# VectorE's exponential with a half-octave cubic, in a new order of the attention kernel

## The chip, the core and the metric

The kernel runs on one core of one Trainium2 chip. The metric is device microseconds of one execution; three timed executions gave a median of 3478.04 us (3476.9 to 3479.99). A trace of one profiled execution tells where the time goes. The engines are TensorE (PE in the profile; its weight loads are PEld), VectorE (DVE), ScalarE (ACT), GpSimd (POOL) and SyncE (SP), which issues DMAs.

## What is computed

Four layers of grouped attention with one key and value head (two sets of weights, used in turn), each with a layer norm before it and a residual sum behind it. There are 2048 rows of width 512, 32 query heads of width 16:

```python
def _A_ref(x, wq, wk, wv, wo):          # H = 32, Dh = 16, S = 2048
    q = (x @ wq).reshape(B, S, H, Dh).transpose(0, 2, 1, 3)
    k = x @ wk
    v = x @ wv
    scores = jnp.einsum("bhqd,bkd->bhqk", q, k) * (Dh ** -0.5)
    p = _softmax(scores, axis=-1)
    o = jnp.einsum("bhqk,bkd->bhqd", p, v)
    return o.transpose(0, 2, 1, 3).reshape(B, S, H * Dh) @ wo
x = A_x
x = x + _A_ref(_layernorm(x), *A);  x = x + _B_ref(_layernorm(x), *B)
x = x + _A_ref(_layernorm(x), *A);  x = x + _B_ref(_layernorm(x), *B)
```

The exponentials of the scores are by far the largest part: 4 layers x 32 heads x 2048 x 2048 of them.

## The kernel before

**Tiles of exponentials.** The scores are cut into 4096 tiles of 128 partitions x 1024 columns. TensorE makes a tile of scores in PSUM, one engine turns it into exponentials in SBUF (`pt`, 16 buffers), and TensorE multiplies these by the values and a column of ones and sums them in two PSUM banks `acc` (the ones give the softmax's denominator).

- 3715 tiles go through ScalarE: `score` (L767) makes a tile in one of two PSUM buffers `st`, and one ACTIVATE at L777 takes the exponential. In what follows such a tile is a **score tile**.
- 381 tiles go through VectorE: `score_v` makes half a tile in the bank `by_v`, `exp_first` (L800) turns it into an integer whose upper bits are the exponent of the result (L809, twice a tile), and then a chain of six passes over 1024 columns follows: cut out the mantissa (L823), keep the exponent (L825), three passes of a polynomial in the mantissa (L826 to L828), and the product (L820). VectorE takes such tiles 24 ahead of ScalarE.

**TensorE in eighths.** The matmuls of attention work on 64 x 32 parts of the array: two halves of 64 rows, and in each four columns of 32. Each half does its own work; below they are half 0 and half 1. `both` (L482) issues four matmuls on a half at a time, at L495. The kinds of steps are:

- the score tile: one group of four on each half;
- a sum into `acc`: `acc[0]` on half 0 only, `acc[1]` on half 1 only, 256 columns, or 512 where the same sum's next step follows at once (`carry` in `step`, L875). These are float32 and stream twice;
- a product step: a piece of a projection (queries, keys and values, outputs) summed into the one bank `beside`, on either half. A product has 12 steps on each half.

**The touch.** The two halves must not sum into one bank at the same time. Where a product goes from one half to the other, `touch` (L904) has VectorE copy one column of `beside` into `seen` (L906): VectorE waits until TensorE has written the bank, and TensorE's next write to `beside` waits for VectorE's copy. All engines run their own instructions in order.

**The order.** `ORDER` (L56) is a string, written out by hand or by a program; the kernel walks it letter by letter, and each letter issues one step: `S` a score tile; `a` to `s` steps on one or both halves (table `STEPS`, L201: for `a` a sum on both halves; `l` a sum on half 0, `m` on half 1; `p` a product step on half 0, `q` on half 1; `b` to `k` mixtures, `r` and `s` half a VectorE tile); `P` and `F` steps on the whole array; `Y` a touch; `I` VectorE's first pass; `0` and `1` the next pass of one of two chains under way; `X`, `G`, `D` VectorE's other work; `Q` a load of queries. So a piece `SaaY0` is a score tile, two sums on both halves, a touch and a pass of a chain.

GpSimd squares queries and keys for a check of their lengths (L440, L416) and takes powers for the layer norm (L376).

Of the kernel before, what the change touches and what calls it, by code (L numbers as in the profile page):

```python
# [11 lines left out]
I32 = mybir.dt.int32  # L12
AF = mybir.ActivationFunctionType
ALU = mybir.AluOpType
# [35 lines left out]
LEAD = 1013283008.0  # L50
C0, C1, C2, C3 = 37.67991256713867, 23.053848266601562, 12.310662269592285, -0.15703019499778748
# [5 lines left out]
    "SSXPPPSPPPQSaSPPPSPPPSXaSXaaSbpSaaSbSbbSpppSaaYScSccScSccSaXQSXamGSmSGFSXlaXSaXXSaXXaSXaXSXaXaSaSamXSXFS"  # L57
    "XaSXQaaXSaSFSXaXSaXSGFGSlXXaXSaSFSXaaXSaSbbSbpSbbSapSaYSQaaScqSaaScGSccSqGqqSmXaXSaXSaXaXSFSXaXXaXSXXaSX"
    "aXaXSXlXXSaaXXSSQaaSXXSFSXaXSaXSGFGSgXaISaXSfXaISFX0SXa0SaXaS0aSF0SaaXSa0SQaaXSa0SbbSlGpSlbGSkbISbSrYaIS"
    "c0c0Sqc0Scc0SeSaXaXSa0SFaXS0QaSaaXSXaaXXSmXGSmXXmXSlXGSgXaISaXXSaXXaSXfXISa0aS0mXSaXa0SFS0aSQaXaS0aSaXaS"  # L60
    "XGSFG0SlaSXaSXafXSIFXSXsaISaXa0Sa0SF0SaaXSa0SQaXSa0aSb0pSalGSppGSbhSIbSkdISaY0aS0c0qScc0ScSc0aSqaXSaXa0S"
    "aQSaXaXSXFSXaXaXXSXmGqSGqcSicIScSjcISaY0mS0bp0Saa0SbpSb0Saa0SQbSbaXSaXaSaSacGSqjGSmIaSiISaa0Sc0q0SccS0aS"
    "aaY0Sbb0SbSQbbSapSpaXSaXaSlGpSkaISbGpShbISb0pS0a0SaaS0cScc0Scc0ScSQaaYSpaXSaXaSaSbbSgGpISpbGShbISd0Sa0aY"
    "0SaSc0cSc0qScc0SaSQeaXSaXSaaSaaSFGSXfSIaXcGSgISa0aS0ap0SaaS0bSaa0SbbXS0bSQaXaSXbDpXSaaYScGScqqGSjqISaaDS"
    "iISaXa0SaXqS0aaXS0mSaXaSXSaaSQaXXSaDSXaaD0SPPPSGPPGSPDrSaIaDS0aSas0SaaISPP0Sf0aISaD0SgaISa0SQaa1Sa0rSaa1"
    "SPGPSGPPDSaXaDSaXSaDppDS0bpSaIl0SakSaIp0SaSh1p0SaaS1aD0SccSIcq0SioISc0SfaYDSa0SbdDSaXaDSaXSaD0aSbpISb0b0"
    "SkbISb0SaaY1Si0qSaa1Sc0SaaD1Scc0ScScIaXSa0SaaXSaDa0SFSaXrDSaIbDSh0SaaISpb0Sg0aISb0Sbb1Sa0Saa1Sj0cScc1Scq"
    "0ScSaIaXSa0SQaaXSa0sSbaISa0kSbGpSGpppISpa0Sh0aISa0Saa1Si0qSccD0ScSc1c0SaSaYIaSD0dSaXa0SfaSIaXSa0aShpDSb0"
    "bSbISb0b0Sa0sSaaYISa0Sfc1Sc0qSaa1Sc0SccISa0qSaaXSa0SaaXSa0kSbIpSb0hSbIpS0a0Sa0aSiqISa0aSi1qSa0Saa1S0bSaY"
    "aISq0cSc0jSaaISc0SaaXSa0SaaXSr0mISQa0SF0SaaXSXaSPPPSPPGPSGsPISaXX0SaaS1a0Saa1Sa0SaaXSa0aSaXSaaXSa0SaPXSf"  # L70
    "aISl0SaaXSP0PSasXSaaISaXSa0aSXrPSaIaXSPSaaSXsXSaIa0SP0PPSa1Sa0rSaa1S0PPPSa1SPPP0SaaISa0SgaISPP0PSaXSa0aS"
    "hpISb0b0Sa0SgaISc0qSic1Sa0Saa1Sb0pSbpISaaY0SjcISc0qSQaaXSa0Shb1Sb0bSaISlGl0SpbGSb0mSaY0SicISc0qSfa1Sc0Sa"
    "aISc0c0SaSaXaSXXaDSaXXaDSaXXSaDXaXSa0sSaIaSXD0mSaaX1Sf0SaaISXaXSF00SaSaXaDSaXSgXmISaD0SflDSFD0SaaXS0SSIa"
    "XSaXaXD0SF0SXaS0aaSXsaISF0SaaXSa0SaaXSa0ShbIS0pa0SaDaS0kbSbIpSDb0rSalYDSc0SQaa1Sc0SaaISa0a0ScScGqqGSqq0S"
    "aaXSaXSaDXa0SaSaX0aSFXSsDaXISaXa0SXa0SaXX0fScIqSc0qScaDS0aSgaISDb0kSbbISbDpS0b0Sa0aSraISc0cSaXSa0aSaXaS0"
    "fScIcS0qc0Sa0sSaaISb0Shb1Sb0pSa1aS0aScIcS0eSaa0SsaISb0bSaXSa0aSaXrSaIa0Sc0Sc0cSm0SgaISb0pShb1Sa0SaaISQc0"
    "qq0ScSa0aSsaISbGpkGSpp0SaaXSa0SaaISaXSaDa0S0jcISc0qScc1Sj0aSa1Sa0aSb1pSaa0SbSbIbD0SkbSIaaY0SiSaXa0SaaISa"
    "XSaDa0SF0SaXa0SjcSIcq0Sic1Sm0Saa1Sb0pSbbISb0ShbISa0SaaY1Sa0Sic1SaXa0SaScIc0SqcSj0cSaaIS0aShb1S0bSaIaS0bb"
    "0SkbISa0SaaYS1Qgq0SeaXSa0SbaISlGpSl0bGSb0ShbISa0pSha1Sa0SaaY1Sc0SaaISc0cSc0SiaSIc0qSaaXSa0ShbISb0pSk0aIS"
    "a0aSa1Si0cScq1Sc0cSc1SaaY0SapSbIb0SaSaXaXXSrDaISaXXaSDaSXXgmDXSXa0SamXS1aXD0SamISa0SaXrSIaaXS0FSaXSa0aSa"  # L80
    "XrSXaDaS0FSXSDXSXXDSF0SISaXa0SaXsSQaIa0Sa0SF1SaXaS0aSaXaS0arSPGPPGSP0PSPPPISa0SaD0aSsaISa0aSaD1Sa0aSa1Sa"
    "0aSa0SfaISP0PSaaDSa0SaaD0SasSaIaDSa0Sg0aISPP0SaaXSaXSa0aSaX0SaaSXa0rSaaISXFS0faISXl0SaX0aSsXSIaaXX0SrSa1"
    "a0SaS1a0SaaIS0SgaISm0Sf1Sa0aSa1Sa0aSlISa0SsaISa0aSr1SQa0aS1Sa0aSGSGlISa0SgaISaD0Saa1Sa0SaaD1Sf0SaaIS0mSa"
    "0SgaISa0SgaDSm0SaaISDm0SaDaS0jcISc0Scc1Sj0qqSaaY1Sb0Sbb1Sbb0SbSaIaXSa0SicISc0Sic1Sa0qSaIaS0qa0SjaSIaq0Sa"
    "aS1a0ShbS1bp0SbbISb0SaaXSa0sSccISc0Sia1Sa0aScISa0a0SjcSaImY0SQhSa1a0Saa1SbGpSpGppS0pbSaIa0SbSaXaDS0scScI"
    "cS0cSi1cSD0aqSaIaY0Sa0ShbSIb0pSgbDSb0SbaXSaXXaDSaXXSaDaXXSa0SalISaXXSa0aXS0fISaX0aSa1Sa0rSaaXSXl0SFSXa0S"
    "aaISaXaSXa0Sa0Sas0SaaISF0SrSX0SISaXaSXaX0Sa0a0SasSaIa0SFS1aXSa0aSaXSa0aSF0SQaXa0SaSaXa0SajSGqqqGScIc0SaS"
# [103 lines left out]
    "mD0Sa0SasSIaa0SaSD1ar0Saa1S0SaaIS0SaaDSs0SaaISaD0SarSDaa0SSIa0aS0sSIa0aSa1Sa0rSaa1S0Saa1SS0aaSI0SaaS0asS"  # L191
    "aISa0fSIlS0ag0SImS0aaS1rS0aaS1aS0aSa1aS0SaaIS0sSaIaS0aSa1rSa0aSISa0a0SsSIaa0SrSGGSl0aSa1Sa0aSaISaD0aS0mS"
    "a0aSsaDISa0Saa1Sr0SaaIS0s0SaaSIDSa0aSaaD0SrSDS0SIa0Sa0Sa0aSa0sSaaISa0Sr1S0SISa0aS0aSa0aSas0SaaISa0SaS0a0"
    "Sa0aSa0SaaS0aSa0aSaSaaSaSaSaaSSaaSSaaSSaaaa"
)


# [1160 lines left out]
```

## Time and profile before

| | |
|---|---|
| median of three timed runs | 3478.04 us (3476.9 to 3479.99) |
| span of the profiled execution, first to last instruction | 3474.3 us |
| its own time | not given apart from its span; the median is 3.7 us above the span |
| TensorE's mean granted clock | 0.998 of full speed |
| score tiles on ScalarE / tiles on VectorE | 3715 / 381 |
| touches | 105 |

The page of the profile gives busy times by engine and by group of instructions. A matmul's duration in it is longer than the time for which it keeps its part of the array from the next one, since matmuls overlap, so the distance from one start to the next says more than the durations. Times in a timeline are counted from the start of the span.

### The profile page before, as it was taken

The page shows a single profiled execution, that of the slowest core. Times are in us where ns is not written, and L with a number is a line of the kernel's source. Part 1 is how long each engine was busy: PE and PEld are TensorE (multiplying, and loading weights), DVE is VectorE, ACT ScalarE, POOL GpSimd, SP SyncE. Part 2 cuts the span into 40 slices and gives each one's busy share as a digit, 9 for nine tenths or more (in the row PEclk, how much of TensorE's full clock was granted, in tenths as well). Part 3 has the DMA queues.
Part 4 walks back from the last instruction along what each step waited for, and adds up shares of the span by engine and source line. Part 5 has one row for each costly group of instructions (what it writes and reads, how often), then busy time and mean ns, then how long its engine had stood idle before and what let it go on. Part 6 is the DMA issues. An engine that isn't in the chain of part 4 may idle for free.

```text
span 3474.3 us, 202688 instructions
## 1 busy us (share of the span) xinstructions
PE 3387.5 (98%) x96011; PEld 2024.7 (58%) x96011; DVE 3305.2 (95%) x4431; ACT 3433.9 (99%) x3745; POOL 167.8 (5%) x137
## 2 busy tenths in 40 slices
PE   9999999999999999999999999999999999999998
PEld 5566566564556656656455665665546666564554
DVE  4889999999989999999998999999999899999997
ACT  8999999999999999999999999999999999999998
POOL 2001000000000000000000100000000000000000
PEclk9999999999999999999999999999999999999999
DMA  3221111110012111111001211111101121110010
GB/s 102 66 78 39 45 45 36 42 39 25 28 45 69 32 44 47 44 28 46 18 30 54 58 42 34 50 36 34 47 14 44 48 54 37 47 44 25 27 37 21
DMA packets 93811, 147.56 MB, mean 42 GB/s; under 512 B 30056, under 2 KB 47976, under 8 KB 92968
## 3 DMA queue, kind: packets, MB, share of 16 engines
q1 hardware_dynamic: 91400, 133.64, 13.0%
q8 instruction: 752, 12.32, 1.5%
q10 hardware_dynamic: 1568, 0.85, 0.1%
q14 instruction: 91, 0.75, 0.1%
HBM read 90.57 MB, written 34.59 MB: 36 GB/s over the span
## 4 chain that ended last, share of the span: by engine, by line
ACT 44%; PE 42%; DVE 10%; issue 2%; DMA 1%; SPq 0%; POOL 0%; DVEq 0%; ACTq 0%; POOLq 0%
ACT pt L777 44%; PE acc L495 22%; PE st L495 11%; PE beside L495 7%; DVE pt L809 2%; DVE poly L828 1%; PE by_v L495 1%; DVE pt L820 1%; DVE poly L826 1%; DVE poly L827 1%; DVE mant L823 1%; DVE pt L825 1%; PE beside L532 1%; DMA qt<-qs 0%; PE beside L389 0%
## 5 line engine op out<-in xcount | busy, mean ns | idle before, releaser
L777 ACT ACTIVATE pt<-st 128x1024 f32<-128x1024 f32 x3715 | 3419.7, 1078 | 12.7 <-PE st L495 10.7
L495 PE MATMUL acc<-pt,vop 64*32 64x256 f32 (+1 forms) x50536 | 2797.5, 440 | 2.9 <-DVE sum L925 1.2
L495 PE MATMUL st<-qt,kop 64*32 64x512 f16 x29720 | 1685.6, 380 | 68.5 <-ACT pt L777 52.4
L495 PEld LDWEIGHTS <-kop 64*32 64x32 f16 x32768 | 795.6, 90 | 1009.1 <-issue 744.1
L495 PEld LDWEIGHTS acc<-pt,vop 64*32 64x32 f32 x50536 | 1227.6, 106 | 259.0 <-issue 8.1
L809 DVE TENSOR_SCALAR pt<-by_v 128x512 int32<-128x512 f32 x762 | 521.2, 684 | 44.4 <-PE by_v L495 30.8
L828 DVE SCALAR_TENSOR_TENSOR poly<-poly,mant 128x1024 f32<-128x1024 f32 x381 | 467.4, 1227 | 0.7
L820 DVE SCALAR_TENSOR_TENSOR pt<-poly,pt 128x1024 f32<-128x1024 f32 x381 | 466.7, 1225 | 0.6
L827 DVE SCALAR_TENSOR_TENSOR poly<-poly,mant 128x1024 f32<-128x1024 f32 x381 | 464.1, 1218 | 1.8
L826 DVE SCALAR_TENSOR_TENSOR poly<-mant 128x1024 f32<-128x1024 f32 x381 | 464.0, 1218 | 0.0
L495 PE MATMUL beside<-wo,ot 64*32 64x512 f16 x5472 | 402.3, 376 | 0.1
L495 PE MATMUL beside<-xnT,wq 64*32 64x512 f16 x5376 | 390.5, 376 | 0.9 <-DVE gv L432 0.7
L495 PE MATMUL by_v<-qt,kop 64*32 64x512 f16 x3048 | 303.8, 377 | 3.0 <-DMA qt<-qs 1.8
L825 DVE TENSOR_SCALAR pt<-pt 128x1024 int32<-128x1024 int32 x381 | 262.0, 688 | 2.7
L823 DVE TENSOR_SCALAR mant<-pt 128x1024 int32<-128x1024 int32 x381 | 261.3, 686 | 1.8
L495 PEld LDWEIGHTS <-ot 64*32 64x32 f16 x5472 | 165.1, 92 | 43.9 <-issue 4.3
L495 PEld LDWEIGHTS <-wq 64*32 64x32 f16 x5376 | 158.0, 92 | 47.5 <-issue 5.5
L440 POOL TENSOR_TENSOR sq<-qs 128x512 bf16<-128x512 f16 x64 | 100.9, 1576 | 934.4 <-DVE qs L437 934.4
L925 DVE COPY sum<-acc 128x512 f32<-128x512 f32 x126 | 82.5, 682 | 14.4 <-PE acc L495 11.7
L376 POOL TENSOR_TENSOR rstd<-var,nhalf 128x4 f32<-128x4 f32 x15 | 28.8, 1918 | 1235.5 <-DVE var L375 1235.5
L495 PE MATMUL beside<-xnT,wkv 64*32 64x512 f16 x1152 | 84.0, 376 | 0.0
L437 DVE TENSOR_SCALAR qs<-beside 128x512 f16<-128x512 f32 x62 | 42.4, 683 | 18.1 <-PE beside L495 7.3
(125 smaller groups left out, 869.7 us busy)
## 6 DMA issues: line engine op xcount, KB each, us to landing
qt<-qs SPq DMA_DIRECT2D x85, 512.0 KB
qs<-qs SPq DMA_DIRECT2D x127, 128.0 KB
rec<-rs SPq DMA_DIRECT2D x63, 256.0 KB
xs<-xt SPq DMA_DIRECT2D x48, 256.0 KB
xt<-xs SPq DMA_DIRECT2D x48, 256.0 KB
sum<-sum SPq DMA_DIRECT2D x252, 32.0 KB
xt<-in_A_x_dram SPq DMA_DIRECT2D x30, 256.0 KB
out_dram<-xt SPq DMA_DIRECT2D x15, 256.0 KB
```

The costliest lines, as they stand in the source:

```text
L437: V.tensor_scalar(qs[:, 0], ps, BIG, -BIG, ALU.min, ALU.max)
L440: G.tensor_tensor(sq, qs[:, 0], qs[:, 0], ALU.mult)
L495: PE.matmul(o[32 * j:32 * j + 32], w[j][h], x[j][h], start=start, stop=stop, skip_group_check=True, tile_position=(64 * r, 32 * j))
L777: e = A.activation(pts[:, i], st[s], AF.Exp, scale=SCALE / UP / UP).ins
L809: w = V.tensor_scalar(e[:, 512 * r:512 * r + 512], by_v, SCALE / UP / UP * LOG2E * 2.0 ** 23, LEAD, ALU.mult, ALU.add).ins
L820: writer[i] = V.scalar_tensor_tensor(p, poly, C0, p, ALU.add, ALU.mult).ins
L823: lambda: V.tensor_scalar(mant.bitcast(I32), e, 0x7FFFFF, 0x3F800000, ALU.bitwise_and, ALU.bitwise_or),
L825: lambda: V.tensor_scalar(e, e, 0x7F800000, None, ALU.bitwise_and),
L826: lambda: V.scalar_tensor_tensor(poly, mant, C3, mant, ALU.add, ALU.mult),
L827: lambda: V.scalar_tensor_tensor(poly, poly, C2, mant, ALU.add, ALU.mult),
L828: lambda: V.scalar_tensor_tensor(poly, poly, C1, mant, ALU.add, ALU.mult),
L925: V.tensor_copy(sums[pr, odd], acc[odd])
```

## The change

**A polynomial with one pass less.** The mantissa is cut at half octaves in place of octaves (masks `0x3FFFFF` and `0x7FC00000`; the bits `HALVES` are put in with the second mask), so that a cubic does: two polynomial passes and the product, five passes in place of six.

**GpSimd on every eighth VectorE tile.** The cubic is written with a shifted mantissa `m + MB`, for which it is `((m + MB)^2 + MA) (m + MB) + MC`. On tiles 8, 24, 40, ... VectorE makes the shift and GpSimd the square; on tiles 16, 32, ... GpSimd does both. VectorE's next pass waits for the square.

**Another order.** All of `ORDER` is new; it has 19577 letters for 14291. By count of the instructions in the two built programs:

| | before | after |
|---|---|---|
| score tiles (ScalarE) | 3715 | 3677 |
| tiles on VectorE | 381 | 419 |
| of these with a square by GpSimd | 0 | 52 |
| touches (`Y`) | 105 | 429 |
| runs of touches with no other VectorE instruction between them | 105 | 219 |
| matmuls of sums into `acc`: 256 / 512 columns wide | 17768 / 7500 | 30408 / 1180 |
| steps on half a product, both halves together | 3000 | 3000 |
| whole-array product steps before the first score tile | 0 | 9 |

```diff
-LEAD = 1013283008.0
-C0, C1, C2, C3 = 37.67991256713867, 23.053848266601562, 12.310662269592285, -0.15703019499778748
+LEAD = 1030161728.0
+C0, C1, C2 = 7.247527122497559, 6.331161975860596, 0.5959731936454773
+HALVES = 0x1A827A
+MB = C2 / 3.0
+MA = C1 - C2 * C2 / 3.0
+MC = C0 - C1 * C2 / 3.0 + 2.0 * C2 ** 3 / 27.0
 ORDER = (
-    "SSXPPPSPPPQSaSPPPSPPPSXaSXaaSbpSaaSbSbbSpppSaaYScSccScSccSaXQSXamGSmSGFSXlaXSaXXSaXXaSXaXSXaXaSaSamXSXFS"
+    "QXPPPPPPPPPSPPPSSXXpppYqSoSYppsnYqqqlISqqeYpSYqqrqYppSIdpmS0lmXlSm0aSXa0lSFXSlmlXmSXlmXSlmXXlmSQlmX0SmaS"
...
+        j = now["tile"] = now["tile"] + 1
+        square = j % 8 == 0
+
         def last():
-            writer[i] = V.scalar_tensor_tensor(p, poly, C0, p, ALU.add, ALU.mult).ins
+            writer[i] = V.scalar_tensor_tensor(p, poly, MC if square else C0, p, ALU.add, ALU.mult).ins
+
+        def first():
+            V.tensor_scalar(mant.bitcast(I32), e, 0x3FFFFF, 0x3F800000, ALU.bitwise_and,
+                            ALU.bitwise_or)
+            if j % 16 == 0:
+                G.tensor_scalar(mant, mant, MB, None, ALU.add)
+                G.tensor_tensor(poly, mant, mant, ALU.mult)
+
+        def masked():
+            V.tensor_scalar(e, e, 0x7FC00000, HALVES, ALU.bitwise_and, ALU.bitwise_or)
+            if j % 16 == 8:
+                V.tensor_scalar(mant, mant, MB, None, ALU.add)
+                G.tensor_tensor(poly, mant, mant, ALU.mult)
+
+        if square:
+            chains.append(deque([
+                first, masked, lambda: None,
+                lambda: V.scalar_tensor_tensor(poly, poly, MA, mant, ALU.add, ALU.mult),
+                last]))
+            return
 
         chains.append(deque([
-            lambda: V.tensor_scalar(mant.bitcast(I32), e, 0x7FFFFF, 0x3F800000, ALU.bitwise_and,
+            lambda: V.tensor_scalar(mant.bitcast(I32), e, 0x3FFFFF, 0x3F800000, ALU.bitwise_and,
                                     ALU.bitwise_or),
-            lambda: V.tensor_scalar(e, e, 0x7F800000, None, ALU.bitwise_and),
-            lambda: V.scalar_tensor_tensor(poly, mant, C3, mant, ALU.add, ALU.mult),
-            lambda: V.scalar_tensor_tensor(poly, poly, C2, mant, ALU.add, ALU.mult),
+            lambda: V.tensor_scalar(e, e, 0x7FC00000, HALVES, ALU.bitwise_and, ALU.bitwise_or),
+            lambda: V.scalar_tensor_tensor(poly, mant, C2, mant, ALU.add, ALU.mult),
             lambda: V.scalar_tensor_tensor(poly, poly, C1, mant, ALU.add, ALU.mult),
             last]))
```

In the new program the lines of the same code are higher by 55 at `both` (L495 is now L550) and L809 is L864, L906 is L983; the chain's passes stand at L901 to L905 and L878, those of the tiles with a square at L881, L888, L890 and L896.

**TensorE around a touch, before.** These are TensorE's instructions around the touch in `SaaY0Sbb0` (the 167th and 168th score tiles), with the semaphores that they wait for; repeated rows are left out. `acc_469` is `acc[0]`, `acc_470` is `acc[1]`.

```order
L495 MATMUL acc_469<-pt,vop_2_107 32x512 x4
L495 MATMUL acc_470<-pt,vop_2_107 32x256 x8
L495 MATMUL st_466<-qt,kop_2_99 32x512 [waits Activation_49]
L495 MATMUL beside<-xnT_1057,wq_183 32x512 [waits DVE_49]
L495 MATMUL acc_470<-pt,vop_2_107 32x256 x4
```

Between the last write to `beside` (before these rows) and the next, which waits for VectorE, stand the sums of two steps on both halves and a score tile.

**TensorE around touches, after.** This is the piece `SYpppYqm`, at the 1968th score tile, and the start of the next score tile.

```order
L550 MATMUL st_466<-qt,kop_2_99 32x512 [waits Activation_49]
L550 MATMUL beside<-xnT_37655,wq_31036 32x512 [waits DVE_49]
L550 MATMUL beside<-xnT_37656,wq_31036 32x512
L550 MATMUL beside<-xnT_37655,wq_31037 32x512
L550 MATMUL beside<-xnT_37655,wq_31037 32x512 [waits DVE_49]
L550 MATMUL acc_470<-pt,vop_1_106 32x256 x4
L550 MATMUL st_465<-qt,kop_2_99 32x512 [waits Activation_49]
```

The three product steps on half 0 and the one on half 1 now follow each other with a touch between them and nothing else; the sum and the next score tile are queued behind the second wait.

**VectorE around touches, before.** A touch stands among the passes of the chains.

```order
L828 SCALAR_TENSOR_TENSOR poly_46947<-poly_46947,mant_46946 128x1024 [waits DVE_49]
L906 COPY seen<-beside 128x1 [waits PE_49]
L825 TENSOR_SCALAR pt<-pt 128x1024 [waits DVE_49]
L820 SCALAR_TENSOR_TENSOR pt<-poly_46947,pt 128x1024 [waits DVE_49]
L809 TENSOR_SCALAR pt<-by_v 128x512
L826 SCALAR_TENSOR_TENSOR poly_47181<-mant_47180 128x1024
```

**VectorE around touches, after.** Here is one of the tiles with a square (L881 to L896 and L878) and the touches around it; the eight touches at L983 in the last two rows are those of five score tiles, the 1967th to the 1971st.

```order
L881 TENSOR_SCALAR mant_47414<-pt 128x1024 [waits DVE_49,Activation_49]
L888 TENSOR_SCALAR pt<-pt 128x1024 [waits DVE_49]
L890 TENSOR_SCALAR mant_47414<-mant_47414 128x1024
L896 SCALAR_TENSOR_TENSOR poly_47415<-poly_47415,mant_47414 128x1024 [waits Pool_49]
L983 COPY seen<-beside 128x1 [waits PE_49]
L878 SCALAR_TENSOR_TENSOR pt<-poly_47415,pt 128x1024 [waits DVE_49]
...
L983 COPY seen<-beside 128x1 [waits PE_49]
L983 COPY seen<-beside 128x1 [waits DVE_49,PE_49] x7
```

VectorE's pass at L896 now stands behind GpSimd's square of the tile just shifted, and whole runs of touches stand together with no pass between them.

More of the change, by code (lines that the diff above doesn't have):

```diff
@@ L195 @@
+    "SlmSIaS0rmlmSIlS0fa1Slm0lSmlSIa0lsSIms0SlmS1lmS1ma0SlS0lmlmSIlm0SrmlSIlmlm0SflS1ml0SmaSIls0SaIlS1smS0maS"
+    "GlSGmm0SllS0maSlImlSDDf0lSIml0mrSlml1Sm0lSmlmS0lSIlmlS0smSIlm0fSlS1lm0lmSS10lmlmS0mlSmlImSl0mSlS0sSIlm0l"
+    "mSg0mlS0mlmSl0mlSmlS0mSDaIaSDlmDrSmaISl0smlISml0rSmIlS0lsmSlm1S0lmlS1mS0lmlmISlm0SrmlSIlm0lmSS1lm0lmSS0l"
+    "m0lmSlm0SaS0maSlaSlmSaaaa"
 )
@@ L735, in fast_path @@
     divs = deque()
-    now = dict(n=0, v=-1, e=0, slot=0, half=None)
+    now = dict(n=0, v=-1, e=0, slot=0, half=None, tile=0)
     group = [0, 0]
```

321 lines of the change are left out of this document (184 added, 137 removed).

## The prediction

> **What bounds the kernel now.** I read the page's busy shares first, then windows of the steady part, then who waits for whom.
>
> ```profile
> span 3474.3 us, 202688 instructions
> PE 3387.5 (98%) x96011; PEld 2024.7 (58%) x96011; DVE 3305.2 (95%) x4431; ACT 3433.9 (99%) x3745; POOL 167.8 (5%) x137
> ```
>
> Three engines look full, so the shares decide nothing. The windows from 200 to 3200 us, and their sum:
>
> ```profile
> 200.00:800.00 600.00, 593.30 (x17296) 359.99 (x17292) 588.82 (x794) 599.75 (x652) 30.58 (x18) 1.00 0.16 46
> 2400.00:3200.00 800.00, 779.00 (x22178) 460.22 (x22163) 775.36 (x1008) 798.27 (x870) 26.60 (x16) 1.00 0.13 39
> sum 3000.00, PE 2941.20 PEld 1769.74 DVE 2914.06 ACT 2990.72 POOL 136.08; mean PE 735.30 PEld 442.43 DVE 728.51 ACT 747.68 POOL 34.02
> ```
>
> The fourth pair of numbers is ScalarE: idle for 9.3 of 3000 us. It is the bound, and its tiles have one length:
>
> ```profile
> L777 ACT ACTIVATE pt<-st 128x1024 f32<-128x1024 f32 x3715 | 3419.7, 1078 | 12.7 <-PE st L495 10.7
> 29.29 33.22 ACT L777 ACTIVATE pt<-st 128x1024 f32<-128x1024 f32 x36
> PE st L495 <- ACT pt L777: 52.4, 144, 0.5
> ```
>
> Busy time over count is 3419.7 / 3715 = 0.9205 us a tile; in a run of 36 the distance is (33.22 - 1.08) / 35 = 0.918 (the mean of 1.078 overlaps the next). ScalarE waited for TensorE for 10.7 us in all, TensorE for ScalarE 144 times. So TensorE keeps up, and the question is by how much. Starts in a timeline show what its steps cost:
>
> ```profile
> 1003.15 0.33 PEld L495 LDWEIGHTS acc<-pt,vop 64*32 64x32 f32 x16
> 1003.36 0.62 PE L495 MATMUL acc<-pt,vop 64*32 64x256 f32 x16
> 1003.79 0.40 PE L495 MATMUL st<-qt,kop 64*32 64x512 f16 x8
> 1004.00 1.05 PE L495 MATMUL acc<-pt,vop 64*32 64x512 f32 x16
> 1004.86 0.41 PE L495 MATMUL st<-qt,kop 64*32 64x512 f16 x8
> ```
>
> A score tile takes 1004.00 - 1003.79 = 0.21 us on both halves, a sum of 256 columns 1003.79 - 1003.36 = 0.43, one of 512 columns 0.86. A product step of 512 columns in f16 takes 0.21, as the score tile does, on its half alone.
>
> **The change part by part.**
>
> *ScalarE.* 38 tiles fewer: 38 x 0.9205 = **-35.0 us**, where ScalarE remains the bound.
>
> *VectorE.* Its rows:
>
> ```profile
> L809 DVE TENSOR_SCALAR pt<-by_v 128x512 int32<-128x512 f32 x762 | 521.2, 684 | 44.4 <-PE by_v L495 30.8
> L828 DVE SCALAR_TENSOR_TENSOR poly<-poly,mant 128x1024 f32<-128x1024 f32 x381 | 467.4, 1227 | 0.7
> L820 DVE SCALAR_TENSOR_TENSOR pt<-poly,pt 128x1024 f32<-128x1024 f32 x381 | 466.7, 1225 | 0.6
> L826 DVE SCALAR_TENSOR_TENSOR poly<-mant 128x1024 f32<-128x1024 f32 x381 | 464.0, 1218 | 0.0
> L825 DVE TENSOR_SCALAR pt<-pt 128x1024 int32<-128x1024 int32 x381 | 262.0, 688 | 2.7
> L906 DVE COPY seen<-beside x105: 140/151/160, 37.2 to 3296.6; 128x1 f32<-128x1 f32 x105
> ```
>
> A tile took 2 x 0.684 + 2 x 0.688 + 4 x 1.22 = 7.6 us and takes 6.4 without GpSimd. By counts: 343 + 14 polynomial passes go (-436 us), 76 first passes (+52), 38 products (+47), 76 masks (+52), 26 shifts at a mask's length (+18) and 324 touches of 0.15 (+49) come: -218 us, to 3087. VectorE is not the bound, so I count this gain at nothing.
>
> *Sums of 256 columns in place of 512.* Per column they cost the same (0.43 and 0.86 above); the more frequent weight loads, 0.33 us for 16, lie under the 0.43 of their matmuls. Nothing; below by nothing, and above by 0.1 us a pair (0.43 - 0.33) if that cover went.
>
> *Nine whole product steps before the first score tile*: 9 x 0.21 = **+1.9 us** before ScalarE's first tile.
>
> *Touches.* This is the term that decides. Before, the touch of the order's first piece above looks so:
>
> ```profile
> 178.80 0.44 PE L495 MATMUL st<-qt,kop 64*32 64x512 f16 x8
> 178.89 0.15 DVE L906 COPY seen<-beside 128x1 f32<-128x1 f32 x1
> 179.01 1.23 DVE L828 SCALAR_TENSOR_TENSOR poly<-poly,mant 128x1024 f32<-128x1024 f32 x1
> 179.10 0.40 PE L495 MATMUL beside<-xnT,wq 64*32 64x512 f16 x4
> 179.11 0.42 PE L495 MATMUL acc<-pt,vop 64*32 64x256 f32 x4
> ```
>
> The touch ends at 179.04; TensorE's next write to `beside` starts 0.06 later. The sum queued behind it, on the other half and with no touch of its own, starts only then too, although the score tile had left both halves at 179.01: what is queued behind a waiting instruction waits as well. Where VectorE is ready, the way there is:
>
> ```profile
> 103.54 0.40 PE L495 MATMUL beside<-xnT,wkv 64*32 64x512 f16 x4
> 103.99 0.16 DVE L906 COPY seen<-beside 128x1 f32<-128x1 f32 x1 [0.35 <-PE beside L495]
> ```
>
> From the start of a product step to the next one behind a touch it is 0.45 + 0.15 + 0.06 = 0.66 us. The step itself takes 0.21, so **0.45 us** of TensorE go to an uncovered touch. Before, all 105 touches are covered: by the order at least five groups (5 x 0.21 = 1.07 us) stand between the two writes. After, 129 of 429 have no other group between the writes, 65 have one and 72 two. The order's second piece, `SYpppYqm`: the score tile covers 0.21 of the first touch, so the product steps start at 0.45 and end at 1.09; the second touch takes 0.45, to 1.54; the step on half 1 ends at 1.75 and the sum on that half at 2.18. ScalarE needs a tile every 0.92.
>
> I added the same lengths up along both whole orders, for each half by itself, with 0.45 us at a touch less what covers it, and ScalarE left out. In groups of six score tiles, and counting only what a group takes above six ScalarE tiles (6 x 0.918), the old order exceeds by 7.8 us in all, close to the 9.3 us for which ScalarE was idle. The new one exceeds by 114 us. Groups of forty give 0 and 60: that is the lower end, as if ScalarE could lie far ahead. It can't, with two buffers of scores, so I take six: 114 - 8 = **+106 us**. With touches at no cost the new order exceeds by 16 us, at 0.2 us by 43.
>
> *GpSimd's squares.* Not in the trace at this size. The nearest rows, and a place where the two engines meet:
>
> ```profile
> L440 POOL TENSOR_TENSOR sq<-qs x64: 1039/1950/1957, 17.8 to 2923.7; 128x512 bf16<-128x512 f16 x64
> 2513.43 1.36 POOL L416 TENSOR_TENSOR ksq<-kop 128x512 bf16<-128x512 f16 x1 [29.99 <-DVE kop L412]
> 2513.95 1.39 DVE L825 TENSOR_SCALAR pt<-pt 128x1024 int32<-128x1024 int32 x1
> ```
>
> A square of 512 columns takes 1.04 us at least and 1.95 in the middle of the row; VectorE's mask, 0.69 elsewhere, takes 1.39 beside one: it stands until GpSimd is done (2514.79). So a square of 1024 columns is about 2 x 1.04 = 2.1 us, in which VectorE's passes stand still too, and in the order above its next pass waits for it anyway. For 52 tiles VectorE loses at most 26 x 2.1 + 26 x 4.2 (shift and square on GpSimd, the shift bounded by a square) = 164 us and saves 26 x 1.22 + 26 x 0.53 = 46 (one pass, or one less a shift). I take no effect on the end, as 3087 + 164 = 3251 us stay below the span; the upper end is in the rivals.
>
> The Trainium skill speaks against this part: "SBUF — State Buffer", section "SBUF: two separate sides", has VectorE and GpSimd share one pair of ports as an exclusive lock, held for a whole instruction, by VectorE in passes with two SBUF inputs or in a two-port mode. The 1.39 us above agrees. By that rule the square is no second engine's work but takes VectorE's time, and I already count it so.
>
> *Sum*: 3474.3 - 35.0 + 1.9 + 106 = 3547 us of span, and with the 3.7 us by which the median lies above the span **3551 us**. Its own range is 3505 (groups of forty: +60) to 3600.
>
> **Rivals.**
>
> *A. The forecast*: the uncovered touches leave ScalarE without scores. For it: order, in-order wait and the 0.45 are each seen above. Against it: no touch of the old order is uncovered, so the sum of the parts is not in this trace.
>
> *B. Faster: ScalarE still sets the pace.* If TensorE's 0.45 us gaps vanish in its lead (it waited for ScalarE 144 times) or the product steps need not wait for the copy, only the 16 us without touches remain: 3474.3 - 35.0 + 1.9 + (16 - 8) + 3.7 = 3453. It decides where a touch costs under 0.2 us. For it: ScalarE was idle for only 0.3% in a trace where VectorE was 97% busy, so late touches were absorbed. Against: those had over 1 us of cover.
>
> *C. The two cancel.* At 0.2 us a touch, 43 - 8 = 35 us eat the 35: 3480.
>
> *D. Slower still: VectorE late.* A touch run starts behind a pass of 1.22 us; half of that, 0.61, for 219 runs is 134 us, and GpSimd's squares hold VectorE up as well. Half of the 134 on top of A gives 3618. For it: squares and touches share VectorE's queue in the order above. Against: where touches are dense the order has no passes at all.
>
> **How the numbers follow.** A 0.56, B 0.23, C 0.08, D 0.13. The predicted time is A's, 3551 us. The range takes in A with its own range, B with its lower end (3443, the 35 us alone) and C: 3443 to 3610; most of D lies beyond. 0.2% (7 us) is about what a measurement of this kernel can tell from no change. Faster is B, 0.23; same is C, 0.08; slower is A and D, 0.69.
>
> **What would show it.** In the profile after: 3677 tiles at L777 with the same 0.92 a tile, and before them an idle time near 115 us, ended by TensorE's scores, in place of 12.7; that idle time in the stretches with runs of touches, and none where pieces have no touch. At the 1968th score tile, about 2.1 us to the next one. VectorE's busy share falls to under 90%, and a square of GpSimd takes about 2.1 us. I am wrong if ScalarE is above 98% busy (B), or if the idle time is ended by sums that wait for VectorE's tiles (D).

## The result, and the profile after

The changed kernel takes **3725.46 us** (median of four runs, 3721.77 to 3731.59) against 3477.49 us of the kernel before on the same chip: a ratio of 1.0717 [1.0702, 1.0732]. It is slower, as predicted, but by 248 us in place of the 73 that the prediction gives, and the time lies above the range, which ends at 3610. Had ScalarE stayed the bound, 3677 score tiles would have given about 3478 - 35 = 3443 us; so there are 3725.5 - 3443 = **283 us** to explain. The profiled execution has a span of 3723.8 us. One execution of a later kernel (4504 us, at a granted clock of 0.75) was in a slower state of the chip and is left out of its median.

From the page of the kernel after: the span, the busy times by engine, and the engines' shares of the chain that ended last.

```profile
span 3723.8 us, 228596 instructions
PE 3537.6 (95%) x108651; PEld 2249.2 (60%) x108651; DVE 3193.6 (86%) x4614; ACT 3449.8 (93%) x3707; POOL 320.8 (9%) x215
PE 53%; DVE 20%; ACT 17%; issue 3%; POOL 3%; DMA 1%; SPq 1%; DVEq 0%; POOLq 0%; ACTq 0%
```

No engine is full any more. Before, ScalarE was busy for 99%, and its share of the chain was 44%; now its share is 17%, and TensorE (42% before) and VectorE (10% before) hold the chain by turns. A chain that goes to and fro between two engines that are 95% and 86% busy suggests that each waits for the other. The groups of the same page (line, engine, operation, out<-in, shape and count, then busy time, mean ns of one, and idle time ahead of them with its main releaser) show who:

```profile
L832 ACT ACTIVATE pt<-st 128x1024 f32<-128x1024 f32 x3677 | 3435.5, 1070 | 249.4 <-PE st L550 231.4
L884 POOL TENSOR_SCALAR mant<-mant 128x1024 f32<-128x1024 f32 x26 | 82.6, 3175 | 884.3 <-DVE mant L881 884.3
L983 DVE COPY seen<-beside 128x1 f32<-128x1 f32 x429 | 67.2, 157 | 253.3 <-PE beside L550 234.7
L891 POOL TENSOR_TENSOR poly<-mant 128x1024 f32<-128x1024 f32 x26 | 54.4, 2091 | 844.5 <-DVE mant L890 844.5
L896 DVE SCALAR_TENSOR_TENSOR poly<-poly,mant 128x1024 f32<-128x1024 f32 x52 | 65.3, 1255 | 68.1 <-POOL poly L885 38.8
L1002 DVE COPY sum<-acc 128x512 f32<-128x512 f32 x126 | 83.6, 686 | 17.3 <-PE acc L550 13.4
```

ScalarE is idle for 249.4 us in place of 12.7, nearly all of it until TensorE has made scores. That row is not the whole loss: busy time over count is 3435.5 / 3677 = 0.934 us in place of 0.9205, since a tile that starts after idle time overlaps no tile before it. That is 0.0135 x 3677 = 50 us more; with the 249.4 - 12.7 = 237 us it makes 287, which is about the 283. VectorE stands 253 us before the touches at L983, 235 of them for TensorE's write to `beside`, and 68 us before the passes behind a square (L896), for GpSimd.

The view of waits (who waited for whom: us in total, times, longest us) shows what TensorE waits for. Rows of the matmul (PE) and of the weight load (PEld) for the same releaser overlap and must not be added.

```profile
ACT pt L832 <- PE st L550: 231.4, 322, 8.4
PE beside L550 <- DVE seen L983: 62.9, 172, 6.4
PE by_v L550 <- DVE pt L864: 26.3, 40, 2.2
PE acc L550 <- DVE sum L1004: 20.5, 3, 7.7
PEld acc L550 <- DVE sum L1002: 21.2, 53, 1.1
PE st L550 <- ACT pt L832: 9.7, 28, 0.5
```

TensorE waited for ScalarE 144 times (52.4 us) before; now 28 times (9.7 us). Its lead is gone. It waits for VectorE at three kinds of places: touches, scores of VectorE's tiles (`by_v`), and copies of sums (L1002, L1004).

**A run of touches** is where the forecast put its term. The timeline at the 1968th score tile (start us, length us, engine, line, operation; in brackets the idle time before and its releaser; `...` stands for rows left out, here and below):

```profile
1989.92 0.16 DVE L983 COPY seen<-beside 128x1 f32<-128x1 f32 x1 [0.93 <-PE beside L550]
1990.13 0.83 PE L550 MATMUL beside<-xnT,wq 64*32 64x512 f16 x12
...
1990.17 1.02 ACT L832 ACTIVATE pt<-st 128x1024 f32<-128x1024 f32 x1 [0.94 <-PE st L550]
1991.01 0.16 DVE L983 COPY seen<-beside 128x1 f32<-128x1 f32 x1 [0.93 <-PE beside L550]
1991.22 0.40 PE L550 MATMUL beside<-xnT,wq 64*32 64x512 f16 x4 [0.26 <-DVE seen L983]
...
1991.26 0.40 PE L550 MATMUL st<-qt,kop 64*32 64x512 f16 x4
...
1991.43 0.61 PE L550 MATMUL acc<-pt,vop 64*32 64x256 f32 x8
...
1991.66 0.16 DVE L983 COPY seen<-beside 128x1 f32<-128x1 f32 x1 [0.50 <-PE beside L550]
...
1992.31 1.02 ACT L832 ACTIVATE pt<-st 128x1024 f32<-128x1024 f32 x1 [1.12 <-PE st L550]
```

The score tiles start 1992.31 - 1990.17 = 2.14 us apart (2.1 predicted). The three product steps start at 1990.13, the last of them 2 x 0.21 = 0.42 later; the copy starts at 1991.01, and TensorE's next write at 1991.22: 0.67 us from the last step's start, as forecast.

**A square** costs in another way. The timeline around one whose shift and square are both GpSimd's:

```profile
2372.53 3.20 POOL L884 TENSOR_SCALAR mant<-mant 128x1024 f32<-128x1024 f32 x1 [1.23 <-DVE mant L881]
...
2375.82 1.89 POOL L885 TENSOR_TENSOR poly<-mant 128x1024 f32<-128x1024 f32 x1
...
2377.74 1.23 DVE L896 SCALAR_TENSOR_TENSOR poly<-poly,mant 128x1024 f32<-128x1024 f32 x1 [4.64 <-POOL poly L885]
2379.00 1.22 DVE L878 SCALAR_TENSOR_TENSOR pt<-poly,pt 128x1024 f32<-128x1024 f32 x1
2380.15 0.68 DVE L864 TENSOR_SCALAR pt<-by_v 128x512 int32<-128x512 f32 x1
2380.75 0.15 DVE L983 COPY seen<-beside 128x1 f32<-128x1 f32 x1
2380.95 0.40 PE L550 MATMUL beside<-xnT,wq 64*32 64x512 f16 x4 [3.54 <-DVE seen L983]
...
2381.60 0.62 PE L550 MATMUL beside<-xnT,wq 64*32 64x512 f16 x4 [0.26 <-DVE seen L983]
```

VectorE stands for 4.64 us at L896. Behind that instruction in its queue stand two passes and a touch, and behind the touch TensorE stands for 3.54 us, and with it the next score tiles. The product step at 2381.60 then takes 0.62 us in place of 0.40: TensorE's granted clock is 0.50 from 2381.3 to 2388.0. The square itself takes what it was expected to take, 1.89 us, but the shift before it 3.20, and what is queued behind the wait stands as well.

**A load of weights** makes the longest stalls, and the prediction has nothing of them. The timeline where output weights (`wo`) come in:

```profile
1127.45 6.71 SPq L379 DMA_DIRECT2D wst<-in_B_wo_dram  x4
...
1131.23 0.43 DVE L395 TENSOR_SCALAR wo<-wst 128x512 f16<-128x512 f32 x1 [6.06 <-DMA wst<-in_B_wo_dram]
...
1136.79 1.28 DVE L1004 TENSOR_TENSOR sum<-acc,sum 128x512 f32<-128x512 f32 x2
...
1137.52 0.65 PE L550 MATMUL acc<-pt,vop 64*32 64x256 f32 x4 [7.72 <-DVE sum L1004]
...
1139.10 1.02 ACT L832 ACTIVATE pt<-st 128x1024 f32<-128x1024 f32 x1 [8.41 <-PE st L550]
```

VectorE waits for the transfer with its first pass over the weights, and twice more, for 0.27 and 1.30 us, for later parts of them. The sum that empties TensorE's bank stands behind these passes, and ScalarE gets its next scores after 8.41 us. In the letters of the two orders, the first pass stands 5 to 8 score tiles behind its load at the seven loads of before (7, 5, 8, 7, 7, 8, 8), and 0 to 5 after (0, 2, 0, 5, 1, 3, 2).

### The profile page after: what moved, and what is told of

The parts are those of the page before. It is cut to its first block, busy times and chain, and to the rows that moved or that the text cites. A ratio compares the mean times of both kernels' runs of the same rounds, so it can differ in the third digit from the quotient of the medians.

```text
span 3723.8 us, 228596 instructions
## 1 busy us (share of the span) xinstructions
PE 3537.6 (95%) x108651; PEld 2249.2 (60%) x108651; DVE 3193.6 (86%) x4614; ACT 3449.8 (93%) x3707; POOL 320.8 (9%) x215
## 4 chain that ended last, share of the span: by engine, by line
PE 53%; DVE 20%; ACT 17%; issue 3%; POOL 3%; DMA 1%; SPq 1%; DVEq 0%; POOLq 0%; ACTq 0%
PE acc L550 26%; ACT pt L832 17%; PE st L550 13%; PE beside L550 11%; DVE pt L864 3%; DVE pt L878 3%; DVE poly L904 2%; DVE poly L905 2%; PE by_v L550 2%; POOL mant L884 1%; DVE mant L901 1%; DVE pt L903 1%; DVE poly L896 1%; DVE seen L983 1%; PE beside L587 1%
## 5 line engine op out<-in xcount | busy, mean ns | idle before, releaser
L832 ACT ACTIVATE pt<-st 128x1024 f32<-128x1024 f32 x3677 | 3435.5, 1070 | 249.4 <-PE st L550 231.4
L550 PE MATMUL acc<-pt,vop 64*32 64x256 f32 (+1 forms) x63176 | 2985.9, 386 | 36.7 <-DVE sum L1004 20.5
L550 PE MATMUL st<-qt,kop 64*32 64x512 f16 x29416 | 1899.6, 381 | 28.0 <-ACT pt L832 9.7
L550 PEld LDWEIGHTS acc<-pt,vop 64*32 64x32 f32 x63176 | 1576.8, 106 | 385.9 <-issue 36.0
L550 PEld LDWEIGHTS <-kop 64*32 64x32 f16 x32768 | 794.9, 90 | 704.2 <-issue 437.2
L864 DVE TENSOR_SCALAR pt<-by_v 128x512 int32<-128x512 f32 x838 | 572.7, 683 | 62.9 <-PE by_v L550 51.4
L550 PE MATMUL beside<-xnT,wq 64*32 64x512 f16 x5856 | 480.6, 382 | 46.5 <-DVE seen L983 38.8
L878 DVE SCALAR_TENSOR_TENSOR pt<-poly,pt 128x1024 f32<-128x1024 f32 x419 | 514.9, 1229 | 4.6
L904 DVE SCALAR_TENSOR_TENSOR poly<-mant 128x1024 f32<-128x1024 f32 x367 | 451.9, 1232 | 0.0
L905 DVE SCALAR_TENSOR_TENSOR poly<-poly,mant 128x1024 f32<-128x1024 f32 x367 | 449.2, 1224 | 3.1
L550 PE MATMUL beside<-wo,ot 64*32 64x512 f16 x4992 | 387.0, 377 | 23.8 <-DVE seen L983 18.3
L550 PE MATMUL by_v<-qt,kop 64*32 64x512 f16 x3352 | 340.6, 380 | 27.6 <-DVE pt L864 26.3
L983 DVE COPY seen<-beside 128x1 f32<-128x1 f32 x429 | 67.2, 157 | 253.3 <-PE beside L550 234.7
L550 PEld LDWEIGHTS <-wq 64*32 64x32 f16 x5856 | 173.4, 92 | 170.2 <-issue 131.7
L901 DVE TENSOR_SCALAR mant<-pt 128x1024 int32<-128x1024 int32 x367 | 256.2, 698 | 10.4
L550 PEld LDWEIGHTS <-ot 64*32 64x32 f16 x4992 | 147.5, 92 | 110.0 <-issue 78.5
L884 POOL TENSOR_SCALAR mant<-mant 128x1024 f32<-128x1024 f32 x26 | 82.6, 3175 | 884.3 <-DVE mant L881 884.3
L495 POOL TENSOR_TENSOR sq<-qs 128x512 bf16<-128x512 f16 x64 | 74.4, 1162 | 891.4 <-DVE qs L492 891.4
L891 POOL TENSOR_TENSOR poly<-mant 128x1024 f32<-128x1024 f32 x26 | 54.4, 2091 | 844.5 <-DVE mant L890 844.5
L896 DVE SCALAR_TENSOR_TENSOR poly<-poly,mant 128x1024 f32<-128x1024 f32 x52 | 65.3, 1255 | 68.1 <-POOL poly L885 38.8
L1002 DVE COPY sum<-acc 128x512 f32<-128x512 f32 x126 | 83.6, 686 | 17.3 <-PE acc L550 13.4
```

The costliest lines, as they stand in the source:

```text
L550: PE.matmul(o[32 * j:32 * j + 32], w[j][h], x[j][h], start=start, stop=stop, skip_group_check=True, tile_position=(64 * r, 32 * j))
L832: e = A.activation(pts[:, i], st[s], AF.Exp, scale=SCALE / UP / UP).ins
L864: w = V.tensor_scalar(e[:, 512 * r:512 * r + 512], by_v, SCALE / UP / UP * LOG2E * 2.0 ** 23, LEAD, ALU.mult, ALU.add).ins
L878: writer[i] = V.scalar_tensor_tensor(p, poly, MC if square else C0, p, ALU.add, ALU.mult).ins
L884: G.tensor_scalar(mant, mant, MB, None, ALU.add)
L896: lambda: V.scalar_tensor_tensor(poly, poly, MA, mant, ALU.add, ALU.mult),
```

## The experiments

Each kernel ran beside the kernel before, which took 3474 to 3476 us there, and the ratios are to that. "After" is the changed kernel, 3725.46 us. Lines move by a few between the kernels.

**The squares, in the new order.** All tiles take VectorE's five passes.

```diff
-        square = j % 8 == 0
+        square = False
```

> The changed kernel with VectorE's own five passes on every tile: the 52 squares (and 26 shifts) of GpSimd are gone, 26 more mantissa products and 26 fewer shifts... in sum 52 more passes of 1.22 us on VectorE. Two theories. T (touches): nearly all of the 248 us lost comes from touches that nothing covers; then GpSimd's share is small and the time stays at 3700 to 3725 us. L (VectorE late): a large part comes from VectorE standing in its queue, and of the 27 gaps of TensorE above 1.5 us (78.5 us in all) some 16 lie beside the pass that waits for a square (L896, 68.1 us of waiting); then the time falls by those 36 us and the smaller gaps of the same kind, to 3640 to 3680 us, and ScalarE's idle time of 249 us before its score tiles falls by the same amount.

3646.58 us, 1.0498 [1.0479, 1.0517]: **79 us** less than after. Its waits:

```profile
ACT pt L832 <- PE st L550: 165.8, 245, 9.0
PE by_v L550 <- DVE pt L864: 5.5, 12, 0.9
```

TensorE's wait for VectorE at `by_v` falls from 26.3 to 5.5 us, ScalarE's for scores from 231.4 to 165.8. So the squares made VectorE late, although it does more work without them (3204.7 us busy for 3193.6).

**Touches that the halves don't need.** Of the 429, 142 stand between two product steps on the same half. They are left out, the squares kept. Three pieces of the order:

```diff
-SYqql
+Sqql
...
-SYpppYqm
+SpppYqm
...
-SmYIlml0
+SmIlml0
```

> The changed kernel without the 142 of its 429 touches that stand between product steps on one and the same half (no switch of halves lies behind them). T: if all touches cost alike, 142 times the 203 us found around touches / 429 = 67 us less, about 3658 us; if the ones left out were the covered ones, 10 to 30 us less. L: touches are not the main term, and at most 20 us go: 3705 us or more. The number of waits of the touch for its product (334 times, 234.7 us) falls by about 142 in both.

3679.46 us (the middle of three executions, 3678.07 to 3686.93), 1.06 [1.0577, 1.0623]: 46 us less, 0.32 for each touch. Neither theory gave this size: it lies between the 3658 and the 3695 us of T.

**Both together.**

> The changed kernel without GpSimd's squares and without the 142 touches that no switch of halves needs: 287 touches are left. If the two losses found so far are separate (79 us for the squares, 42 us for these touches), their sum goes: 3725 - 79 - 42 = 3604 us. If touches were late mainly because they queued behind VectorE's passes that waited for squares, the two overlap, and it stays at 3620 us or more.

3615.01 us, 1.0395 [1.0378, 1.0413]: 110 us less, where 79 + 46 = 125 would be the sum. The two overlap a little, perhaps because a touch behind a square waits anyway.

**The cubic in the old order**, without and with the squares. The old order has a letter more for each chain than the cubic has passes; an empty pass takes that letter, and with a square two are empty.

```diff
-        square = j % 8 == 0
+        square = False
...
+            lambda: None,
             lambda: V.scalar_tensor_tensor(poly, mant, C2, mant, ALU.add, ALU.mult),
```

> The half-octave cubic alone in the order of before (3715 score tiles, 105 touches, six letters a VectorE tile of which one is empty), without GpSimd's squares. T and L agree: the polynomial is no part of the loss; VectorE loses 381 passes of 1.22 us and ScalarE keeps its 3715 tiles and its 12.7 us of idle time, so 3465 to 3480 us. A third theory, that the new passes themselves (the mask with an OR, the 22-bit mantissa) make VectorE late, would give 3500 us or more.

> As the one before, but with GpSimd's square on every eighth VectorE tile (47 of them), in the order of before, where two empty letters stand between the masks and the pass that needs the square. T: GpSimd costs nothing, within 10 us of the kernel without squares. L: each square holds VectorE up by 1 to 3 us and part of that reaches ScalarE: 20 to 80 us more than without squares.

3471.19 us without squares, 0.9992 [0.9983, 1.0002]: no change, though VectorE's busy time falls from 3305.2 to 2908.9 us. It wasn't the bound. With 47 squares 3478.66, 1.0012 [1.0002, 1.0022]: 7.5 us for them, not 79. The rows of the square in the waits of that kernel:

```profile
DVE poly L845 <- POOL poly L834: 6.5, 3, 2.9
DVE poly L845 <- POOL poly L840: 2.0, 1, 2.0
```

Four waits of the 47 tiles with a square, 8.5 us, where the kernel after has 68.1 us for 52: with two empty letters between, other instructions of VectorE stand between the square and the pass that needs it. So the same operations cost 7.5 us in one order and 79 in the other. How much of this is the shorter wait and how much what is queued behind it was not separated.

**Weights loaded earlier.** The first two of a weight's four parts are fetched eight of VectorE's side steps (letter `X`) sooner, which by the order puts 37 to 63 score tiles between the load and the first pass. The passes, and the loads of the other two parts, stay where they were.

```diff
-                work.add_dve("wl", lambda: (load_w(key, 0), load_w(key, 1)), 0)
+                work.ahead[len(work.dve) - 8] = key
+                work.add_dve("wl", lambda: None, 0)
...
             elif what == "X":
+                if work.done_dve in work.ahead:
+                    key = work.ahead.pop(work.done_dve)
+                    for c in range(2):
+                        load_w(key, c)
                 work.step_dve()
```

> The changed kernel with nothing altered but the loads of the first two of four parts of each weight matrix, which are issued eight steps of VectorE's side work earlier. In the order of before five to eight score tiles stood between the load and the first pass on it; in the new order none to three in five cases of seven. Theory W: VectorE waits there for the DMA (L395, 13.8 + 12.1 + 3.1 us), the sums of acc queue behind, and TensorE stands 29 us in four gaps of 6.8 to 8.3 us and runs slower for some us after each; the third and fourth part still come late, so about half of it goes: 15 to 30 us less, 3695 to 3710 us. T (all of it touches): no change, 3725 us.

> The kernel without squares and needless touches, and with the weight loads eight side steps earlier. If weights and the rest are separate, the 28 us that the early loads brought alone come off again: 3615 - 28 = 3587 us. If the stalls at the weights only stood in for other waits: 3600 us or more. What is then left above 3443 us is the needed touches and whatever else the new order holds.

In the kernel after: 3697.37 us, 1.0636 [1.0618, 1.0654], 28 less, and the longest wait of ScalarE for scores falls from 8.4 to 5.9 us. With squares and needless touches gone as well: 3611.86, 1.0391 [1.0375, 1.0407], only 3 less than without. A third pair of kernels below gives 19. Why the same edit brings 28, 3 or 19 us stays open.

**Fewer changes of half.** Product steps swap halves so that the halves change 181 times for 394, with 139 touches for 287. The second kernel loads the weights early too.

```diff
-SpppYqmSYppYqml
+SppppmSYqqqml
```

> As the kernel without squares and without needless touches, but product steps that stand alone in the order change halves so that a product goes from one half to the other as seldom as can be: 181 switches in place of 394, and 139 touches in place of 287. T (a touch that nothing covers costs 0.45 us): up to 148 x 0.45 = 67 us less than with 287 touches, so 3540 to 3560 us. Rival P (what counts is that sums and product steps on opposite halves run side by side, which these swaps break): 3600 us or more.

> The last one with the earlier weight loads too: the 15 to 30 us of W come off whatever that one gives. If squares, touches and weights are all of the 248 us, it comes near what 3677 score tiles allow, 3443 to 3500 us; if something else holds the new order back, 3520 us or more.

3641.92 us, 1.0481 [1.0463, 1.0498]: **27 us slower** with half the touches; with early weights 3622.91, 1.0422 [1.0405, 1.044]. The wait of touches for TensorE falls, and that of VectorE's tiles for scores doubles. In the kernel with both edits, and in this one:

```profile
DVE seen L981 <- PE beside L548: 189.3, 217, 2.7
DVE pt L862 <- PE by_v L548: 57.6, 101, 2.2
```

```profile
DVE seen L980 <- PE beside L547: 114.5, 79, 5.5
DVE pt L861 <- PE by_v L547: 115.6, 135, 3.7
```

Counting touches alone doesn't price an order. A likely reason, not shown by itself: swapped steps no longer stand beside a step on the other half, and a half that has nothing queued stands still.

**A longer touch.** Each of the 287 touches copies 256 columns.

```diff
-    seen_by_v = one.tile([P, 1], F32, name="seen")
+    seen_by_v = one.tile([P, 256], F16, name="seen")
...
-        V.tensor_copy(seen_by_v, beside[:, 0:1])
+        V.tensor_copy(seen_by_v, beside[:, 0:256])
```

> The kernel without squares and needless touches (3615 us), each of its 287 touches made longer: it copies 256 columns in place of one. By the rows for one column (0.16 us) and for 512 columns of PSUM (0.69 us) that is some 0.27 us more a touch, 77 us in all. T (a needed touch lies wholly on the path to ScalarE's next tile): 50 to 77 us more, 3665 to 3692 us; then 287 touches of 0.45 us also account for most of what still lies above 3443. Rival R (most touches are covered, other waits hold the order back): under 30 us more.

3705.57 us, 1.0658 [1.0642, 1.0674]: 90.6 more than with short ones, 0.32 for each. The copy itself takes 0.423 us for 0.156, which is 0.27 more. So these touches are on the path with their whole length, and cost a little more than that; the time is above what either theory expected (3692 at most).

**No touch at all.** Half 1's product steps multiply zero weights into the odd sums' bank, so that only half 0 writes `beside`. That leaves half 1's share of every product out of the result, and the flag in which the kernel judges the ranges of its values is set to zero.

```diff
+            if r:
+                return ("acc", 1), acc[1], cols(none), [x] * 4, ("acc", 1) not in wrote, False
-            return "beside", beside, cols(w), [x] * 4, first, last
+            return "beside", beside, cols(w), [x] * 4, n == 0, n == 3 * NC - 1
...
-            V.tensor_scalar(flag, ok[0][0:1, 4:5], -1.0, 1.0, ALU.mult, ALU.add)
+            V.memset(flag, 0)
```

> The changed kernel with squares and weights as they are, and no touch at all: product steps on half 1 use weights of zero and add to the bank of the odd sums, which only half 1 writes, so that no switch of halves has to be ordered (half 1's share of every product is left out, and the verdict on the ranges is set to good). TensorE issues the same matmuls in the same order. T2 (all 429 touches cost about twice the 106 us forecast): 3725 less 170 to 200, so 3525 to 3555 us. F (the forecast's term was right, and something else holds the order back): 3725 less 100, so 3620 us or more.

> The control: the kernel without squares and needless touches (3615 us), with half 1's product steps in the other bank as in the last one, and its 287 touches kept. If the other bank in itself changes nothing: 3605 to 3625 us. If sums now wait for product steps, or half 0 runs ahead of half 1: that much more or less.

> No squares, no touch at all (half 1's product steps in the other bank), weight loads eight steps earlier. If squares, touches and weights are the whole loss: what 3677 score tiles allow and a few us, 3443 to 3470 us, below the time before. If the order has another fault (sums, transposes and by_v waits with nothing between): 3490 us or more.

Without any touch, squares kept: 3575.88 us, 1.029 [1.0273, 1.0307], **150 us** less than after, between the two expectations. The control (other bank, 287 touches kept, no squares) took 3539.42, 1.0183 [1.0166, 1.02], 76 less than the kernel with both edits, so it fails as a control: with half 1 in another bank its steps no longer stand behind a touch, and 76 us go though the copies stay. That suggests that the cost lies in the instructions behind the wait more than in the copy, and it means that the 150 belongs to touch and shared bank together. With touches, squares and late weights all gone: 3520.06, 1.0133 [1.0116, 1.015], still 77 above 3443. Two of its waits:

```profile
ACT pt L834 <- PE st L549: 71.2, 96, 5.4
PE acc L549 <- DVE sum L1006: 10.9, 10, 3.3
```

What remains is again TensorE late with scores. Some of its waits for sums may be this kernel's own, as product steps share the sums' bank.

**The copies of sums.** To see whether the 126 first copies of a bank of sums have cover, each is made twice: in the new order (with both edits) and in the old one (with the cubic).

```diff
                 V.tensor_copy(sums[pr, odd], acc[odd])
+                V.tensor_copy(sums[pr, odd], acc[odd])
```

> The kernel without squares and needless touches (3615 us) with each of the 126 first copies of a bank of sums made twice (0.69 us more each, 87 us of VectorE in all; the result is the same). G (the copies stand uncovered: TensorE's next sum waits for them): 40 to 87 us more, 3655 to 3700 us. Rival (they are covered, and what is left is elsewhere): 3630 us or less.

> The same doubling in the cubic in the order of before (3471 us). If the old order covers these copies: 3471 to 3480 us. If not: as much more as in the new order.

New order: 3699.62 us, 1.065 [1.0628, 1.0672], 85 more, 0.67 for each copy of 0.69. Old order: 3520.45, 1.0128 [1.0111, 1.0145], 49 more, 0.39 each. TensorE's wait for the second copy, in the new and in the old order:

```profile
PE acc L548 <- DVE sum L1001: 43.0, 84, 1.4
```

```profile
PE acc L499 <- DVE sum L953: 20.0, 48, 1.3
```

In the new order next to nothing covers a second copy of sums, in the old one nearly half of it is covered. That the first copies are uncovered too, and so part of the 77, is argued from this and not shown: in the kernel without touches TensorE's matmuls wait 7.9 + 10.9 us for them. The rest of the 77 stays open.

**A better version was looked for**: the old order's product steps and sums with the cubic and 69 or 70 touches, and VectorE's part planned anew for more tiles on VectorE (404, 402 and 400 for 381). The second begins a tile only where VectorE is less far behind. The third begins a tile at least eight score tiles behind its load of queries, and only 20 tiles ahead of ScalarE (the second cut below).

```diff
-SXamGSmSGFSXlaXSaXXSaXXa
+SrXamGSImSGFSXlaXSsaXXSI0aXXa
```

```diff
-AHEAD = 24
+AHEAD = 20
```

> The cubic in the order of before, of which only VectorE's part is planned anew: five letters a tile with no empty one, no squares, and 404 VectorE tiles in place of 381 (3692 score tiles for 3715); product steps, sums, weights and their distances stay as they were, 70 touches, all with groups between the writes. Theory C (the cubic's gain is real where the order keeps its cover): 23 x 0.92 = 21 us less than the cubic in the unaltered old order, some of it lost where score tiles are left out, so 3452 to 3465 us. Rival: the two by_v halves of a tile now stand closer together and TensorE waits for VectorE there: 3475 us or more.

> As the last one with 402 VectorE tiles and a stricter rule (a tile is begun only where VectorE is under 1 us behind in the plan, 1.5 us before). Theory C: 3455 to 3468 us, 2 us more than the last for the tiles, or less than it if VectorE's lateness counts. Rival: 3475 us or more.

> The old order with VectorE's part planned anew, now with 400 VectorE tiles, each begun at least eight score tiles after the load of its queries and 20 in place of 24 tiles ahead. If the 77 us of waiting for queries were the loss of the last two (and the slower clock after each stall): 3460 to 3480 us. If the closer halves were: 3540 us or more.

3623.58 us (1.043 [1.0416, 1.0444]) and 3617.6 (1.0409 [1.0395, 1.0423]): tiles stood right behind their queries' transfer, which the waits of the first show:

```profile
ACT pt L783 <- PE st L501: 116.6, 91, 8.6
PE by_v L501 <- DMA qt<-qs: 58.2, 21, 7.1
```

With the distance kept, 3555.46, 1.0237 [1.022, 1.0255]: of those waits 0.7 us is left, and it is still slower than before by 80 us. The cause of these 80 stays open. No version was found that beats the kernel before.

## Why the prediction was right and wrong

**Right**: ScalarE's price of a tile and their number; that uncovered touches leave ScalarE without scores and make the kernel slower; the price of such a touch. Over the touches with no other group between the writes (129 by the order, 127 of them found in the trace), from the last step's start to the next write it is 0.45 + 0.16 + 0.05 = 0.66 us in the middle, as forecast, and the one run of touches that was worked out took 2.14 us for 2.1. VectorE's busy share is 86% (under 90% predicted), a square takes 1.9 to 2.1 us, and VectorE's saved pass is worth nothing by itself (3471.19).

**Wrong, first step: "GpSimd's squares ... I take no effect on the end".** They cost 79 us by themselves, 3679 - 3615 = 64 where the needless touches are gone, and a part of 56 where all touches are gone. The step compared VectorE's busy total with the span (3251 below 3474). But a total has no place. At a square VectorE stands up to 4.64 us, and TensorE's touches and bank copies stand behind it. In the old order, with two empty letters behind a square, such squares cost 7.5. Rival D named it, but without a price for the squares: its 67 us on top of the forecast are for touches behind a pass, in 219 runs (VectorE's rows of the kernel after have 153 such runs, not 219). It was laid aside with 0.13; its mechanism came beside A and not instead of it. The bound of the shift by a square was too low as well: it takes 3.2 us on average, not 2.1 at most.

**Wrong, second step: the touches' term, +106 us.** The mechanism was right, the size too small: of the 114 us of the new order 114 - 16 = 98 are for touches, and all touches are worth 150 us (with the caveat on the bank), the 142 needless ones 46. The sum added up TensorE alone and took VectorE to be ready at each touch. TensorE's matmuls waited up to 6.4 us at a touch in the kernel after, where the sum has 0.45; how the excess divides between a late VectorE and ScalarE's two buffers of scores no run shows.

**Wrong, third step: "With touches at no cost the new order exceeds by 16 us".** With no touch, no square and early weights 77 us remain above 3443. The sum of the lengths holds waits of TensorE at touches only. Copies of sums at VectorE are not in it, and in the new order a second copy of 0.69 us adds 0.67; what the first copies take of the 77 is not shown.

**Left out: weights and their transfers.** The change moves every step, and of a moved step its DMAs count too. The prediction never asked how far a pass over weights stands from its load: 0 to 5 score tiles in place of 5 to 8. Earlier loads of half of the parts bring 28 us by themselves, 3 or 19 in the other kernels.

In one line of kernels, 3725 - 3576 = 150 us go with the touches, 3576 - 3520 = 56 with squares and late weights together (no run splits these), and 77 remain. The parts overlap: by themselves they give 150, 79 and 28.

**What would show it**: ScalarE is 93% busy, so B is out, and its idle time ends with score tiles, not with sums. That idle time was predicted near 115 us and is 249.4. It was to lie in pieces with touches, with none elsewhere; counted from the starts of its tiles, 304 us lie above 0.918 a tile, 175 of them in pieces with a touch and 129 in pieces without. That alone speaks against A as the whole story.

## What to carry to other kernels

Price a new order by cover, not by busy totals: every way from TensorE to VectorE (or GpSimd, or a DMA) and back needs other work between its two ends, and what stands behind the waiting instruction in the same queue waits too. List all such round trips before pricing any (touches, handed-over passes, evacuations of sums, the first use of a load), and compare each one's distance before and after. A step that hands work to another engine can save busy time on the first one and still make it late.

## What the runs showed of the hardware

- GpSimd's addition of one constant to 128x1024 float32 (the shift, L884) takes 3.18 us on average, longer than the product of two such tiles (L891, 2.09).
- A pass of VectorE can stand still beside a square: at 1381.71 us of the kernel after a pass at L904 takes 2.90 us, where the row's mean is 1.23.

```profile
1381.60 1.94 POOL L885 TENSOR_TENSOR poly<-mant 128x1024 f32<-128x1024 f32 x1
...
1381.71 2.90 DVE L904 SCALAR_TENSOR_TENSOR poly<-mant 128x1024 f32<-128x1024 f32 x1
```

- TensorE's two halves start on their own. In the piece at the 1968th score tile the sum on half 1 is queued ahead of the next score tile, but that tile's four matmuls on half 0 start at 1991.26 and the sum on half 1 at 1991.43.
- A long stall costs more than its length. The windows around the stall at the weights (window, its length, then busy time and count of PE, PEld, DVE, ACT and POOL, TensorE's granted clock, DMA share, GB/s):

```profile
1120.00:1129.00 9.00, 9.00 (x277) 5.76 (x270) 3.57 (x6) 8.74 (x11) 1.04 (x1) 1.00 0.31 73
1129.00:1137.50 8.50, 0.80 (x20) 0.19 (x13) 4.59 (x9) 1.69 (x2) 0.00 (x0) 0.68 0.42 131
1137.50:1142.00 4.50, 4.48 (x88) 2.50 (x96) 3.79 (x4) 2.05 (x2) 0.00 (x0) 0.50 0.02 4
1142.00:1146.00 4.00, 4.00 (x145) 2.78 (x132) 2.77 (x6) 3.48 (x4) 0.00 (x0) 0.96 0.43 137
```

The granted clock is 0.50 for 4.5 us after the stall, and the matmul of 256 columns takes 0.63 us for 0.40 there. The Trainium skill, "TensorE: Matmul & The Clock Gate", Part 1 ("What's actually happening"), states half clock after an idle window of some 3.4 us and full clock after about as long a time of work. The row agrees on the half clock; its 4.5 us of work are somewhat longer than the page's figure. Over the whole kernel the mean granted clock is 0.992 in place of 0.998, so an estimate of what the clock can take of the 283 us is 0.008 x 3724 - 0.002 x 3474 = 23 us at most; it would be a part of what squares, touches and late weights cost, and was not measured by itself.
